# Batch 0 of an attention and MoE kernel: chunk 1 of w_in loaded before the second x, the order of TensorE's work changed, zero matmuls widened

## The chip, the core and the metric

The kernel runs on one core of a Trainium2 chip. Time is device microseconds (us) of that core; less is better. A profile is one execution of the program, taken by the hardware profiler. The engines have names used throughout: PE is TensorE's matmul, PEld its weight load, DVE is VectorE, ACT is ScalarE, POOL is GpSimd, SP is SyncE. Each has its own queue and works through it in order; engines wait for each other through semaphores.

## What is computed

Eight batches of x (8 heads, 512 positions, 64 values) attend to a state of 32 rows and the state attends to x; the 544 rows of each batch go through a two-layer network with SiLU.

```python
def _attn_ref(x, state):               # B, H, S, Ns, D = 8, 8, 512, 32, 64
    scores = scale * np.matmul(x, state.transpose(0, 1, 3, 2))
    ...                                # softmax over the state's rows: a
    xread = np.matmul(a, state)
    scores2 = scale * np.matmul(state, x.transpose(0, 1, 3, 2))
    ...                                # softmax over the positions: a2
    sread = np.matmul(a2, x)
    return np.concatenate([xread, sread], axis=2)

def _moe_ref(x, w_in, w_out):          # 4352 rows; w_in 512 x 2048, w_out 2048 x 512
    h = x @ w_in
    g = h * (1.0 / (1.0 + np.exp(-h)))
    return g @ w_out
```

## The kernel before

All matrix work is in bf16 with fp32 sums in PSUM. PSUM is used as eight named banks: o0, o1, w0, w1, h0, h1, a0, a1. The order of the program is written by hand; no scheduler moves anything, and semaphores follow from what each instruction reads and writes.

Batch b needs these steps. `cast_x` makes bf16 of the loaded x (eight casts, one for each kt and half); `x_T` transposes it on PE and `x_Te` copies the result to xT; `sc` makes the scores against the state, `ex` takes their exponentials on ACT, `norm_s` and `norm_m` divide by the sums. `a_T` transposes the normalised weights, with a copy to aT. Since the state has only 32 rows, the state is multiplied into w_in first: `w1_m(b, j)` makes chunk j (512 of the 2048 columns) of W1 from the state and chunk j of w_in, in two PSUM banks, and `w1_e` copies the two halves to SBUF. `W1x` is both, here with DVE copying bank a0 and ACT bank a1. `g1(b, ft)` then is two matmuls (one for each half) of W1's block ft with aT into bank h0 or h1, by turns, and ACT's SiLU into g; four blocks ft make one chunk. `G2(0, ft)` adds block ft of g times w_out into the four banks o0, o1, w0, w1, four matmuls. `sread_m`, `sread_n` and `sread_t` make the state's read of x, and x_T, sc and a_T share the banks a0 and a1 with it. `x_T`, `sc` and `ex` of two kt go together in batch 1 and later (`xTs`, `scs`, `exs`).

Batch 0 is the ramp: loads arrive, batch 0's network runs while batch 1's softmax and W1 are made, and PE takes all of it in the order in which the program has it. `warm(n, bk)` puts n matmuls of zeros, 128 columns wide, into a bank that is free. From phase 1 on (`phase(k, fill)`), PE goes through 64 G2 matmuls of batch k, step 16*tt+ft, and the table `fill` inserts the work of the next batches behind chosen steps: `att_tail(fill, b, s, a0, sg, dg)` puts the transposes a_T of batch b at step a0 and its sixteen g1 from step sg on, dg steps apart. In these phases ACT copies aT.

Loads: x of batch 0 goes out on SP's queue in four pieces. The weights, in four chunks each of w_in and w_out, and x of batches 1 and 2 go out on POOL's queue, whose DMA instructions convert fp32 to bf16 on the way for weights. POOL also works: two of batch 0's `norm_m` and the casts for kt 3 of x1 stand in the same queue, and a DMA issue behind them waits for them.

Of the kernel before, what the change touches and what calls it, by code (L numbers as in the profile page):

```python
# [9 lines left out]
BF16 = mybir.dt.bfloat16  # L10
# [9 lines left out]
def kernel(  # L20
# [8 lines left out]
    nc = tc.nc  # L29
# [8 lines left out]
        tc.tile_pool(name="psum", bufs=1, space=bass.MemoryType.PSUM)  # L38
    )

    zeros = pers.tile([128, 128], BF16, name="zeros")
    ident = pers.tile([128, 128], BF16, name="ident")
    st0_f = pers.tile([128, 128], FP32, name="st0_f")
    st_nat = pers.tile([128, B, 128], BF16, name="st_nat")
# [43 lines left out]
    def load_x(b, eng, kt=0, n=4):  # L88
        dst = x_f[b % 2][:, ds(kt, n)].rearrange("p k h e -> p (k h) e")
        eng.dma_start(dst, x_src(b, kt, n))  # L90
# [35 lines left out]
    def x_T(b, kt, bk):  # L126
        v = bf(bk).rearrange("p (k c t) -> p k c t", k=2, c=4)
        for c in range(4):
            nc.tensor.transpose(  # L129
                v[:, kt % 2, c, :], x_n[b % 2][:, kt, c, ds(2, 128)], ident[:]  # L130
            )

    def x_Te(b, kt, n, bk, eng):
        v = bf(bk).rearrange("p (k c t) -> p k c t", k=2, c=4)
        cp(eng, xT[b % 2][:, ds(kt, n)], v[:, ds(kt % 2, n)])
# [154 lines left out]
        cp(eng, t[:, c0:c1], bank[bk][:, c0:c1])  # L290
        (q or nc.sync).dma_start(o_dst(b, tt, c0, c1), t[:, c0:c1])

    def warm(n, bk):
        for i in range(n):
            nc.tensor.matmul(
                bank[bk][:, 0:128], zeros[:], zeros[:], start=True, stop=True,
                skip_group_check=True,
            )

    with tc.manual_schedule():  # L300
# [11 lines left out]
        load_wi(0)  # L312
        load_wo(0)
        load_st(1)
        load_x(1, nc.gpsimd, 0, 2)
        load_x(1, nc.gpsimd, 2, 2)
        warm(20, "o0")

        XB = ("o0", "o1", "w0", "w1")
        SB = ("h0", "h1", "a0", "a1")  # L320
# [6 lines left out]
        def G2(b, ft):  # L327
            for tt in range(4):
                g2(b, tt, ft, OB[tt])
# [22 lines left out]
        cast_x(0, "dve", (1,))  # L352
        st_T(0, "a1", "act", "dve")
        cast_x(0, "dve", (2, 3))
        for kt in range(KT):
            if kt < 3:
                x_T(0, kt + 1, XB[kt + 1])
                x_Te(0, kt + 1, 1, XB[kt + 1], ("act", "act", "dve")[kt])
            sc(0, kt, SB[kt])
            ex(0, kt, 1, SB[kt])  # L360
            if kt == 1:
                warm(6, "o0")
        norm_s(0, 0, 2)
        norm_m(0, "pool", 0, 2)
        norm_s(0, 2, 2)
        norm_m(0, "dve", 3, 1)
        norm_m(0, "pool", 2, 1)
        nc.scalar.preload_act_table(SILU)
        warm(10, "o0")
        w1_m(0, 0, ("w0", "w1"))  # L370
        w1_e(0, 0, ("w0", "w1"), ("act", "act"))
        a_T(0, (("a0", "dve"), ("a1", "dve")))
        load_wi(1)
        load_wo(1)
        load_wi(2)

# [7 lines left out]
        G2(0, 1)  # L384
        sread_t(0, "a1", "dve")
        G2(0, 2)
        cast_x(1, "dve", (0, 1, 2))
        cast_x(1, "pool", (3,))
        load_wo(2)
        load_wi(3)  # L390
        load_wo(3)
        load_x(2, nc.gpsimd)
        for b in range(2, B):
            load_st(b)
        xTs(1, 0, "dve")
        G2(0, 3)
        xTs(1, 1, "act")
        scs(1, 0)
        scs(1, 1)
        exs(1)  # L400
        norm_s(1)
        norm_m(1, "dve")

        W1x(0, 1, AB, DA)
        W1x(1, 0, HB, DA)
        nc.scalar.preload_act_table(SILU)
        a_T(1, (("a0", "dve"),))
        g1(0, 4)
        g1(0, 5)
        g1(0, 6)  # L410
        W1x(1, 1, AB, DA)
        g1(0, 7)
        G2(0, 4)
        g1(1, 0)
        G2(0, 5)
        g1(1, 1)
        G2(0, 6)
        W1x(0, 2, AB, DA)
        g1(1, 2)
        G2(0, 7)  # L420
        g1(1, 3)

        g1(0, 8)
        W1x(1, 2, AB, DA)
        g1(0, 9)
        g1(0, 10)
        g1(0, 11)
        G2(0, 8)
        g1(1, 4)
        G2(0, 9)  # L430
        g1(1, 5)
        G2(0, 10)
        W1x(0, 3, AB, DA)
        g1(1, 6)
        G2(0, 11)
        g1(1, 7)

        g1(0, 12)
        W1x(1, 3, AB, DA)
        g1(0, 13)  # L440
        g1(0, 14)
        G2(0, 12)
        g1(0, 15)
        G2(0, 13)
        g1(1, 8)
        G2(0, 14)
        g1(1, 9)
        G2(0, 15)
        g1(1, 10)
        for tt in range(4):  # L450
            o_e(0, tt, OB[tt], "dve")
        cast_x(2, "pool", (2, 3))
# [47 lines left out]
        add(fill, 8, L(sread_t, 1, "a1", "dve"))  # L500
        add(fill, 8, L(cast_x, 3, "pool"))
        att_head(fill, 2, 9, 17)
        att_tail(fill, 2, 20, 43, 46, 1.1)
        att_head(fill, 3, 48, 58)
        phase(1, fill)

        for k in range(2, 7):
            fill = {}
            if k + 2 < B:
                load_x(k + 2, nc.sync)  # L510
            att_tail(fill, k + 1, 0, 24, 28, 2.15)
            if k + 2 < B:
                add(fill, 0, L(cast_x, k + 2, "pool"))
                att_head(fill, k + 2, 42, 56)
            phase(k, fill)
# [45 lines left out]
```

## Time and profile before

| | us |
|---|---|
| median of 3 runs | 240.18 |
| lowest, highest | 239.5, 241.35 |
| the profiled execution | 239.66 |
| its span, first to last instruction | 237.9 |
| around the span (239.66 - 237.9) | 1.76 |
| busy in the span: PE, ACT, DVE, POOL | 222.2, 138.3, 83.8, 43.9 |

Times in the profile count from the start of the span. A row of a timeline is one or more equal instructions in sequence: start, time until the last of them ends, engine, source line, operation, the tiles written and read, their number, and in brackets the idle time of the engine ahead of it with what ended it. PE's matmuls overlap, so that eight of them can be shorter than eight times one; what one costs in a row is the distance of the starts. PEclk is the clock that TensorE was granted, as a share of 2.4 GHz; 0.50 is 1.2 GHz.

### The profile page before, as it was taken

To read this page: it belongs to the slowest core of one execution; us is meant where nothing else is said; L and a number is where in the kernel's file an instruction comes from. 1 tells how busy PE (TensorE), PEld (TensorE's weight loads), DVE (VectorE), ACT (ScalarE), POOL (GpSimd) and SP (SyncE) were. 2 spreads that over 40 slices of the span, in tenths; PEclk is the share of its full clock that TensorE was granted. 3 is DMA by queue.
4 is the path that set the end of the run, shared out by engine and by line. 5 is a ranking of instruction groups with operands and counts; after the bars stand their busy time and mean duration, and the time that the engine had idled before them with its cause. 6 is when DMAs were issued, how large, how long until landed. Compare 5 with 4: busy or idle time off the path is not lost.

```text
span 237.9 us, 4311 instructions
## 1 busy us (share of the span) xinstructions
PE 222.2 (93%) x1764; PEld 111.2 (47%) x1764; DVE 83.8 (35%) x162; ACT 138.3 (58%) x224; POOL 43.9 (18%) x79
## 2 busy tenths in 40 slices
PE   5797399999999999999999999999999999999993
PEld 4644143444544534453445444544454444466552
DVE  4626622116663164225423461436142711111110
ACT  3652756566467795668565766576657766533210
POOL 4648212000340007000700052003400300000000
PEclk9999679999999999999999999999999999999999
DMA  6999990007511053113411261117101121011112
GB/s 187 156 272 204 207 263 2 1 0 209 192 47 44 3 156 110 47 44 96 171 44 47 61 206 47 41 46 225 44 3 44 47 88 43 15 66 57 44 48 88
DMA packets 18309, 22.08 MB, mean 93 GB/s; under 512 B 3056, under 2 KB 13552, under 8 KB 18288
## 3 DMA queue, kind: packets, MB, share of 16 engines
q1 hardware_dynamic: 11040, 14.81, 19.0%
q0 software_dynamic: 6688, 6.52, 14.9%
q10 hardware_dynamic: 560, 0.46, 0.6%
q8 instruction: 14, 0.23, 0.4%
q14 instruction: 7, 0.06, 0.1%
HBM read 17.30 MB, written 8.91 MB: 110 GB/s over the span
## 4 chain that ended last, share of the span: by engine, by line
PE 85%; ACT 5%; DMA 4%; DVE 3%; issue 1%; POOL 0%; ACTq 0%
PE ps_o L270 44%; PE ps_h L246 24%; PE ps_w L270 3%; DMA w_in_sb<-in_moe_w_in_dram 3%; PE ps_h L257 3%; PE ps_a L129 3%; ACT aT L82 3%; PE ps_w L225 2%; PE ps_a L182 2%; DMA st_f<-in_state_dram 1%; PE ps_a L192 1%; PE ps_a L140 1%; PE ps_h L225 1%; ACT g L254 1%; PE ps_a L225 1%
## 5 line engine op out<-in xcount | busy, mean ns | idle before, releaser
L270 PE MATMUL ps_o<-w_out_sb,g 128*128 128x512 bf16 x480 | 131.2, 379 | 0.0
L254 ACT ACTIVATE g<-ps_h 128x512 bf16<-128x512 f32 x128 | 76.0, 598 | 47.3 <-PE ps_h L246 46.5
L246 PE MATMUL ps_h<-aT,W 128*128 128x512 bf16 x256 | 77.2, 389 | 2.1 <-ACT aT L82 1.6
L270 PEld LDWEIGHTS <-g 128*128 128x128 bf16 x512 | 47.5, 98 | 49.6 <-issue 2.9
L78 DVE COPY o_sb<-ps_o 128x512 f32<-128x512 f32 x30 | 20.5, 685 | 70.7 <-PE ps_o L270 70.7
L246 PEld LDWEIGHTS <-W 128*128 128x128 bf16 x256 | 25.1, 100 | 33.3 <-issue 8.0
L166 POOL TENSOR_TENSOR an<-en,rs 128x1024 bf16<-128x1024 bf16 (+2 forms) x8 | 13.3, 1665 | 96.2 <-DVE rs L162 96.2
L80 POOL CAST x_n<-x_f 128x256 bf16<-128x256 f32 x46 | 16.2, 400 | 39.9 <-PE ps_a L140 26.3
L78 DVE CAST W<-ps_w 128x512 bf16<-128x512 f32 x24 | 15.4, 683 | 1.8 <-PE ps_w L225 1.6
L82 ACT ACTIVATE W<-ps_h 128x512 bf16<-128x512 f32 x25 | 13.7, 603 | 0.5 <-PE ps_h L225 0.5
L78 DVE COPY xT<-ps_a 128x1024 bf16<-128x1024 bf16 x13 | 9.0, 690 | 11.5 <-PE ps_a L129 9.1
L265 ACT ACTIVATE g_s<-ps_h 128x256 bf16<-128x256 f32 x16 | 6.1, 383 | 11.6 <-PE ps_h L257 11.6
L161 DVE TENSOR_REDUCE rs<-en 128x32 f32<-128x1024 bf16 (+1 forms) x9 | 9.9, 1098 | 7.2 <-ACT en L151 7.2
L82 ACT ACTIVATE aT<-ps_a 128x1024 bf16<-128x1024 bf16 x6 | 6.1, 1023 | 10.4 <-PE ps_a L182 10.4
L129 PEld LDWEIGHTS <-x_n 128*128 128x128 bf16 x128 | 8.9, 103 | 6.9 <-DVE x_n L78 3.9
L78 DVE COPY sbd<-ps_a 64x128 bf16<-64x128 bf16 x15 | 4.3, 289 | 20.3 <-PE ps_a L118 20.1
L151 ACT ACT_TABLE_LOAD x7 | 9.0, 1283 | 3.2 <-PE ps_a L140 3.1
L257 PE MATMUL ps_h<-xsT,w_in_sb 128*128 128x256 bf16 x64 | 9.6, 273 | 0.0
L270 PE MATMUL ps_w<-w_out_sb,g 128*128 128x512 bf16 x32 | 9.5, 379 | 0.0
L78 DVE CAST W<-ps_a 128x512 bf16<-128x512 f32 x6 | 4.1, 690 | 14.7 <-PE ps_a L225 14.7
L129 PE MATMUL ps_a<-ident,x_n 128*128 128x128 bf16 x112 | 8.7, 219 | 0.6 <-DVE x_n L78 0.6
L151 ACT ACTIVATE en<-ps_a 128x512 bf16<-128x512 f32 (+1 forms) x16 | 8.4, 568 | 1.0 <-PE ps_a L140 0.9
(59 smaller groups left out, 140.5 us busy)
## 6 DMA issues: line engine op xcount, KB each, us to landing
out_dram<-o_sb SPq DMA_DIRECT2D x32, 256.0 KB, 2.3
x_f<-in_x_dram SPq DMA_DIRECT2D x5, 1024.0 KB, 6.7
w_in_sb<-in_moe_w_in_dram POOLq DMA_DIRECT2D x4, 512.0 KB, 10.1
w_out_sb<-in_moe_w_out_dram POOLq DMA_DIRECT2D x4, 512.0 KB, 9.9
x_f<-in_x_dram SPq DMA_DIRECT2D x4, 256.0 KB, 3.7
x_f<-in_x_dram POOLq DMA_DIRECT2D x2, 512.0 KB, 9.5
x_f<-in_x_dram POOLq DMA_DIRECT2D x1, 1024.0 KB, 15.6
out_dram<-o_sb ACTq DMA_DIRECT2D x1, 256.0 KB, 3.3
```

What stands on the lines that cost most here:

```text
L78: nc.vector.tensor_copy(dst, src)
L80: nc.gpsimd.tensor_copy(dst, src)
L82: nc.scalar.activation(dst, src, func=COPY, bias=0.0)
L129: nc.tensor.transpose(v[:, kt % 2, c, :], x_n[b % 2][:, kt, c, ds(2, 128)], ident[:])
L151: nc.scalar.activation(en[b % 2][:, :, :, ds(kt, n), :].rearrange("p c h k s -> p k (c h) s"), v[:, ds(kt % 2, n)], func=EXP, bias=0.0, sc ...
L161: nc.vector.tensor_reduce(v, en[b % 2][:, :, :, ds(kt, n), :], axis=AX, op=ADD)
L166: e.tensor_tensor(an[b % 2][:, :, :, ds(kt, n), :].rearrange("p c h k s -> p (c h) k s"), en[b % 2][:, :, :, ds(kt, n), :].rearrange("p c ...
L225: nc.tensor.matmul(bank[bks[half]][ds(32 * kt, 32), :], sbd[ds(64 * half, 64), b, kt, half, :], w_in_sb[ds(64 * half, 64), kt, ds(512 * j, ...
L246: nc.tensor.matmul(bk[:], W1[b % 2][:, half, ds(128 * ft, 128)], aT[b % 2][:, half, :, :], start=(half == 0), stop=(half == 1), skip_group ...
L254: nc.scalar.activation(g[b % 2][:, ft, :], bk[:], func=SILU, bias=0.0)
L257: nc.tensor.matmul(bk[:, 0:256], w_in_sb[:, kt, ds(128 * ft, 128)], xsT[:, kt, :, :, :], start=(kt == 0), stop=(kt == KT - 1), skip_group_ ...
L270: nc.tensor.matmul(bank[bk][:, c0:c1], src[:, ft, ds(128 * tt, 128)], w_out_sb[:, ft, c0:c1], start=(ft == 0), stop=(ft == 15), skip_group ...
```

## The change

The zeros tile becomes 512 columns wide and `warm` takes a width. In batch 0's softmax the loop is written out, with zero matmuls at other places and 28 in place of 20 at the start; ahead of the first W1 stand four of 512 columns in place of ten of 128, and two more stand between `a_T(0)` and the first g1. On POOL's queue chunk 1 of w_in is issued where x1's two halves were, and these behind the two `norm_m`. On PE, W1x(0,1), G2(0,3), g1(0,4) to g1(0,7) and W1x(1,0) now stand ahead of batch 1's transposes, and G2(0,4) to G2(0,7) behind its scores; W1x(1,0) uses a0 and a1 in place of h0 and h1; the rest of batch 0 is reordered. In the phases, `a_T` and the g1 get other steps: 42, 48 and 1.0 apart in phase 1 in place of 43, 46 and 1.1; 30 and 2.05 apart later in place of 28 and 2.15.

```diff
@@ -38,7 +38,7 @@
         tc.tile_pool(name="psum", bufs=1, space=bass.MemoryType.PSUM)
     )

-    zeros = pers.tile([128, 128], BF16, name="zeros")
+    zeros = pers.tile([128, 512], BF16, name="zeros")
     ident = pers.tile([128, 128], BF16, name="ident")
     st0_f = pers.tile([128, 128], FP32, name="st0_f")
     st_nat = pers.tile([128, B, 128], BF16, name="st_nat")
@@ -290,10 +290,10 @@
         cp(eng, t[:, c0:c1], bank[bk][:, c0:c1])
         (q or nc.sync).dma_start(o_dst(b, tt, c0, c1), t[:, c0:c1])

-    def warm(n, bk):
+    def warm(n, bk, w=128):
         for i in range(n):
             nc.tensor.matmul(
-                bank[bk][:, 0:128], zeros[:], zeros[:], start=True, stop=True,
+                bank[bk][:, 0:w], zeros[:, 0:128], zeros[:, 0:w], start=True, stop=True,
                 skip_group_check=True,
             )

@@ -312,9 +312,8 @@
         load_wi(0)
         load_wo(0)
         load_st(1)
-        load_x(1, nc.gpsimd, 0, 2)
-        load_x(1, nc.gpsimd, 2, 2)
-        warm(20, "o0")
+        load_wi(1)
+        warm(28, "o0")

         XB = ("o0", "o1", "w0", "w1")
         SB = ("h0", "h1", "a0", "a1")
@@ -352,25 +351,35 @@
         cast_x(0, "dve", (1,))
         st_T(0, "a1", "act", "dve")
         cast_x(0, "dve", (2, 3))
-        for kt in range(KT):
-            if kt < 3:
-                x_T(0, kt + 1, XB[kt + 1])
-                x_Te(0, kt + 1, 1, XB[kt + 1], ("act", "act", "dve")[kt])
+        warm(4, "w1")
+        x_T(0, 1, XB[1])
+        x_Te(0, 1, 1, XB[1], "act")
+        sc(0, 0, SB[0])
+        ex(0, 0, 1, SB[0])
+        warm(3, "w1")
+        x_T(0, 2, XB[2])
+        x_Te(0, 2, 1, XB[2], "act")
+        sc(0, 1, SB[1])
+        ex(0, 1, 1, SB[1])
+        x_T(0, 3, XB[3])
+        x_Te(0, 3, 1, XB[3], "dve")
+        warm(2, "o0")
+        for kt in (2, 3):
             sc(0, kt, SB[kt])
             ex(0, kt, 1, SB[kt])
-            if kt == 1:
-                warm(6, "o0")
         norm_s(0, 0, 2)
         norm_m(0, "pool", 0, 2)
         norm_s(0, 2, 2)
         norm_m(0, "dve", 3, 1)
         norm_m(0, "pool", 2, 1)
         nc.scalar.preload_act_table(SILU)
-        warm(10, "o0")
+        warm(4, "o0", 512)
         w1_m(0, 0, ("w0", "w1"))
         w1_e(0, 0, ("w0", "w1"), ("act", "act"))
         a_T(0, (("a0", "dve"), ("a1", "dve")))
-        load_wi(1)
+        warm(2, "o0", 512)
+        load_x(1, nc.gpsimd, 0, 2)
+        load_x(1, nc.gpsimd, 2, 2)
         load_wo(1)
         load_wi(2)

@@ -384,69 +393,68 @@
         G2(0, 1)
         sread_t(0, "a1", "dve")
         G2(0, 2)
-        cast_x(1, "dve", (0, 1, 2))
+        W1x(0, 1, AB, DA)
+        G2(0, 3)
+        g1(0, 4)
+        cast_x(1, "dve", (0, 1))
         cast_x(1, "pool", (3,))
+        g1(0, 5)
+        W1x(1, 0, AB, DA)
+        g1(0, 6)
+        cast_x(1, "dve", (2,))
         load_wo(2)
         load_wi(3)
         load_wo(3)
         load_x(2, nc.gpsimd)
         for b in range(2, B):
             load_st(b)
+        g1(0, 7)
         xTs(1, 0, "dve")
-        G2(0, 3)
         xTs(1, 1, "act")
         scs(1, 0)
         scs(1, 1)
         exs(1)
         norm_s(1)
         norm_m(1, "dve")
-
-        W1x(0, 1, AB, DA)
-        W1x(1, 0, HB, DA)
         nc.scalar.preload_act_table(SILU)
-        a_T(1, (("a0", "dve"),))
-        g1(0, 4)
-        g1(0, 5)
-        g1(0, 6)
-        W1x(1, 1, AB, DA)
-        g1(0, 7)
         G2(0, 4)
-        g1(1, 0)
         G2(0, 5)
-        g1(1, 1)
         G2(0, 6)
         W1x(0, 2, AB, DA)
-        g1(1, 2)
         G2(0, 7)
-        g1(1, 3)

         g1(0, 8)
-        W1x(1, 2, AB, DA)
         g1(0, 9)
+        a_T(1, (("a0", "dve"),))
         g1(0, 10)
+        W1x(1, 1, AB, DA)
         g1(0, 11)
         G2(0, 8)
+        g1(1, 0)
+        G2(0, 9)
+        g1(1, 1)
+        W1x(1, 2, AB, DA)
+        G2(0, 10)
+        g1(1, 2)
+        G2(0, 11)
+        g1(1, 3)
+        W1x(0, 3, AB, DA)
         g1(1, 4)
-        G2(0, 9)
         g1(1, 5)
-        G2(0, 10)
-        W1x(0, 3, AB, DA)
-        g1(1, 6)
-        G2(0, 11)
-        g1(1, 7)

         g1(0, 12)
+        g1(0, 13)
         W1x(1, 3, AB, DA)
-        g1(0, 13)
         g1(0, 14)
         G2(0, 12)
         g1(0, 15)
         G2(0, 13)
-        g1(1, 8)
+        g1(1, 6)
         G2(0, 14)
-        g1(1, 9)
+        g1(1, 7)
         G2(0, 15)
-        g1(1, 10)
+        for ft in range(8, 11):
+            g1(1, ft)
         for tt in range(4):
             o_e(0, tt, OB[tt], "dve")
         cast_x(2, "pool", (2, 3))
@@ -500,7 +508,7 @@
         add(fill, 8, L(sread_t, 1, "a1", "dve"))
         add(fill, 8, L(cast_x, 3, "pool"))
         att_head(fill, 2, 9, 17)
-        att_tail(fill, 2, 20, 43, 46, 1.1)
+        att_tail(fill, 2, 20, 42, 48, 1.0)
         att_head(fill, 3, 48, 58)
         phase(1, fill)

@@ -508,7 +516,7 @@
             fill = {}
             if k + 2 < B:
                 load_x(k + 2, nc.sync)
-            att_tail(fill, k + 1, 0, 24, 28, 2.15)
+            att_tail(fill, k + 1, 0, 24, 30, 2.05)
             if k + 2 < B:
                 add(fill, 0, L(cast_x, k + 2, "pool"))
                 att_head(fill, k + 2, 42, 56)
```

POOL's queue, from the first weight load on: the rows of before. w_in_sb and w_out_sb are the weights, an_74 is batch 0's normalised softmax, x_f_67 and x_n_69 are x of batch 1 before and after its cast.

```order
L96 DMA w_in_sb<-in_moe_w_in_dram 128x4x512
L101 DMA w_out_sb<-in_moe_w_out_dram 128x4x512
L104 DMA st_nat<-in_state_dram 128x2x64
L90 DMA x_f_67<-in_x_dram 128x4x256 x2
L166 TENSOR_TENSOR an_74<-en_72,rs_76 128x8x64
L166 TENSOR_TENSOR an_74<-en_72,rs_76 128x8x32
L96 DMA w_in_sb<-in_moe_w_in_dram 128x4x512
L101 DMA w_out_sb<-in_moe_w_out_dram 128x4x512
L96 DMA w_in_sb<-in_moe_w_in_dram 128x4x512
L80 CAST x_n_69<-x_f_67 128x4x64 x2
```

The same stretch of POOL's queue in the change:

```order
L96 DMA w_in_sb<-in_moe_w_in_dram 128x4x512
L101 DMA w_out_sb<-in_moe_w_out_dram 128x4x512
L104 DMA st_nat<-in_state_dram 128x2x64
L96 DMA w_in_sb<-in_moe_w_in_dram 128x4x512
L166 TENSOR_TENSOR an_74<-en_72,rs_76 128x8x64
L166 TENSOR_TENSOR an_74<-en_72,rs_76 128x8x32
L90 DMA x_f_67<-in_x_dram 128x4x256 x2
L101 DMA w_out_sb<-in_moe_w_out_dram 128x4x512
L96 DMA w_in_sb<-in_moe_w_in_dram 128x4x512
L80 CAST x_n_69<-x_f_67 128x4x64 x2
```

The second load of w_in and the two loads of x1 have changed places around the two multiplies; all that follows is as it was.

DVE's queue, from the state's read of batch 0 (xsT) to batch 1's aT_79, before. W_80 is W1 of batch 0 and W_81 of batch 1, xT_71, rs_77 and an_75 belong to batch 1's softmax, and ps_a_100 and ps_h_98 are banks a0 and h0.

```order
L78 COPY xsT<-ps_a_101 128x4x32
L78 CAST x_n_69<-x_f_67 128x4x64 x6
L78 COPY xT_71<-ps_a_100 128x1024
L161 TENSOR_REDUCE rs_77<-en_73 128x32
L162 RECIPROCAL rs_77<-rs_77 128x32
L166 TENSOR_TENSOR an_75<-en_73,rs_77 128x1024
L78 CAST W_80<-ps_a_100 128x512
L78 CAST W_81<-ps_h_98 128x512
L78 COPY aT_79<-ps_a_100 128x1024
```

The same stretch of DVE's queue in the change:

```order
L78 COPY xsT<-ps_a_101 128x4x32
L78 CAST W_80<-ps_a_100 128x512
L78 CAST x_n_69<-x_f_67 128x4x64 x4
L78 CAST W_81<-ps_a_100 128x512
L78 CAST x_n_69<-x_f_67 128x4x64 x2
L78 COPY xT_71<-ps_a_100 128x1024
L161 TENSOR_REDUCE rs_77<-en_73 128x32
L162 RECIPROCAL rs_77<-rs_77 128x32
L166 TENSOR_TENSOR an_75<-en_73,rs_77 128x1024
L78 CAST W_80<-ps_a_100 128x512
L78 COPY aT_79<-ps_a_100 128x1024
```

The casts of W1(0,1) and W1(1,0) have moved ahead of and between the casts of x1, and the cast behind the softmax multiply is now that of W1(0,2).

## Rows read from the trace of the kernel before

**Rows 1.** Stages: length, busy time of PE, PEld, DVE, ACT, POOL; PEclk, DMA, GB/s.

```profile
16.12:19.35 3.23, 3.23 (x47) 1.37 (x45) 1.71 (x6) 0.80 (x2) 2.13 (x4) 1.00 1.22 203
...
22.30:25.70 3.40, 0.93 (x14) 0.49 (x11) 0.00 (x0) 3.34 (x4) 1.03 (x3) 1.00 1.24 206
25.70:29.20 3.50, 1.05 (x15) 0.25 (x15) 3.43 (x5) 2.37 (x3) 1.15 (x2) 0.50 1.24 206
29.20:32.50 3.30, 3.28 (x14) 1.50 (x13) 1.26 (x2) 1.12 (x2) 0.71 (x1) 0.50 1.18 292
32.50:54.38 21.88, 21.49 (x130) 8.84 (x130) 4.34 (x7) 13.71 (x26) 1.43 (x4) 1.00 0.21 34
```

**Rows 2.** Timeline of PE, chosen rows up to 37 us.

```profile
0.99 2.32 PE L295 MATMUL ps_o<-zeros 128*128 128x128 bf16 x20 [0.99 <-DVE zeros L305]
...
11.35 0.63 PE L225 MATMUL ps_w<-w_in_sb,sbd 64*32 64x512 bf16 x8 [0.72 <-DMA w_in_sb<-in_moe_w_in_dram]
12.02 1.03 PE L182 MATMUL ps_a<-ident,an 128*128 128x128 bf16 x8
13.14 3.14 PE L246 MATMUL ps_h<-aT,W 128*128 128x512 bf16 x8
16.12 0.59 PE L270 MATMUL ps_o<-w_out_sb,g 128*128 128x512 bf16 x2
...
29.22 1.01 PE L182 MATMUL ps_a<-ident,an 128*128 128x128 bf16 x8 [2.45 <-DVE W L78]
30.03 2.69 PE L246 MATMUL ps_h<-aT,W 128*128 128x512 bf16 x6
...
33.44 0.59 PE L270 MATMUL ps_o<-w_out_sb,g 128*128 128x512 bf16 x2
33.87 0.59 PE L270 MATMUL ps_w<-w_out_sb,g 128*128 128x512 bf16 x2
...
36.98 0.41 PE L225 MATMUL ps_a<-w_in_sb,sbd 64*32 64x512 bf16 x8
```

**Rows 3.** Timelines of ACT and DVE, chosen rows up to 29 us.

```profile
12.03 1.09 ACT L82 ACTIVATE W<-ps_w 128x512 bf16<-128x512 f32 x2 [0.75 <-PE ps_w L225]
...
22.25 1.02 ACT L82 ACTIVATE xT<-ps_a 128x1024 bf16<-128x1024 bf16 x1 [5.33 <-PE ps_a L129]
...
24.58 1.09 ACT L151 ACTIVATE en<-ps_a 128x512 bf16<-128x512 f32 x2
...
18.93 2.41 DVE L78 CAST x_n<-x_f 128x256 bf16<-128x256 f32 x6
...
25.70 1.22 DVE L161 TENSOR_REDUCE rs<-en 128x32 f32<-128x1024 bf16 x1 [3.76 <-ACT en L151]
...
28.49 0.68 DVE L78 CAST W<-ps_a 128x512 bf16<-128x512 f32 x1
```

**Rows 4.** POOL's timeline; among it an issue at 11.91: KB landed, us to landing.

```profile
11.91 0.79 POOL L96 DMA_DIRECT2D w_in_sb<-in_moe_w_in_dram  x1
...
w_in_sb<-in_moe_w_in_dram POOLq DMA_DIRECT2D x1, 512.0 KB, 8.5
...
17.22 0.74 POOL L80 CAST x_n<-x_f 128x256 bf16<-128x256 f32 x2 [3.02 <-DMA x_f<-in_x_dram]
...
25.44 0.71 POOL L104 DMA_DIRECT2D st_nat<-in_state_dram  x1 [1.80 <-DMA w_in_sb<-in_moe_w_in_dram]
27.99 0.70 POOL L104 DMA_DIRECT2D st_nat<-in_state_dram  x1 [1.84 <-DMA w_out_sb<-in_moe_w_out_dram]
```

**Rows 5.** Groups from 33 to 54 us: busy us, mean ns, idle before.

```profile
L254 ACT ACTIVATE g<-ps_h 128x512 bf16<-128x512 f32 x20 | 11.5, 602 | 6.3 <-PE ps_h L246 6.3
```

**Rows 6.** Groups of DVE, from 18.8 to 21.4 us and from 56 to 60.

```profile
L78 DVE CAST x_n<-x_f 128x256 bf16<-128x256 f32 x6 | 2.4, 468 | 0.0
...
L78 DVE CAST x_n<-x_f 128x256 bf16<-128x256 f32 x4 | 0.9, 281 | 0.0
```

**Rows 7.** Waits of PE from 54 us on: us in total, times, longest.

```profile
PE ps_h L246 <- ACT aT L82: 1.6, 6, 0.4
```

## The prediction

> **What bounds the kernel now.** I read the page first. By its table of engines TensorE (PE) is busy for nearly the whole span and no other engine for two thirds of it. The view by stages says where the rest lies: from 22.30 to 25.70 PE works 0.93 of 3.40 us, from 25.70 to 29.20 1.05 of 3.50, while from 32.50 to 54.38 it works 21.49 of 21.88 [rows 1]. So two things can move the end: holes and low clock before phase 1 starts at 54.38, and small PE waits after it. The other engines are hidden under PE.
>
> What fills the holes is read from the PE timeline [rows 2] and the timelines of ACT and DVE [rows 3]. Batch 1's softmax is one chain: transposes, ACT's copy of xT at 22.25 (1.02 us), the load of the exp table behind it, two exps at 24.58 (1.09), DVE's sum at 25.70 with the reciprocal and the multiply behind it, a W cast at 28.49 (0.68), and only then PE's a_T at 29.22, which had waited 2.45. PE has nothing else in its queue: second-chunk work of batch 0 needs w_in's chunk 1, whose issue on POOL's queue stands behind both halves of x1 (issued 11.91, 8.5 us to landing, so 20.4), while x1 is whole at 17.2 [rows 4].
>
> **The clock.** The granted clock is 0.50 (1.2 GHz) from 25.7 to 32.5 [rows 1]; ahead of that PE had been mostly idle. At the start the column reads 1.00, but the rows contradict it: eight transposes take 1.03 us at 12.02, as at 29.22 under 0.50 (1.01), and eight W1 matmuls take 0.63 at 11.35 against 0.41 at 36.98, where the clock is 1.00 [rows 2]. So PE runs at the low level until g1 begins, and at the high one by 16.12, where two G2 matmuls take 0.43, as at 33.44 (to 33.87) [rows 2].
>
> **The change, part by part.** Times of the new kernel are on the old trace's axis.
>
> *To the first G2.* w_in's chunk 0 still lands at 11.3: nothing ahead of it on a queue changes. The softmax of batch 0 may end a little before that, so w1_m still starts at 11.35. What the zero matmuls can change is the clock there. If it is high by about 13 us: w1_m takes 0.41, ACT's two W copies (1.09 as at 12.03 [rows 3]) run 11.8 to 12.9, and g1 starts at 12.9 instead of 13.14. Four g1 of 0.43 over two banks, each bank freed by an activation of 0.60 [rows 5], put the third at 14.2, the fourth at 14.7 and G2 at 15.1 instead of 16.12. That is 1.0 us. If the clock rises only as it did before, the two wide zeros between a_T and g1 (0.43 us each at the low level: four times the 0.11 of a 128-column one, from 20 in 2.32 [rows 2]) start g1 at 13.7 and G2 at about 16.6: 0.5 lost. I take the first: the zeros ahead of w1_m grow from 36 x 128 columns to 37 x 128 plus 4 x 512, and 28 of them in place of 20 stand ahead of the first transpose.
>
> *The filled hole.* The 3.23 us from 16.12 to 19.35, G2, the state's read and two G2, all of it PE work [rows 1], now run 15.1 to 18.3. w_in chunk 1 and x1 change places in the DMA queue, and a chunk is read as 512 by 512 fp32 values, as many as x1 has; so I let them change landings: chunk 1 at 17.2, x1 at 20.4 [rows 4]. Chunk 1 is then there in time, and W1x(0,1) (0.45 with its gaps), G2(0,3) (0.87), g1 4 and 5 (0.87), W1x(1,0) (0.45) and g1 6 and 7 (0.87) follow, to 21.8.
>
> *The chain, put behind that.* DVE now does in order: W cast (ends 19.4), four x casts, W cast, two x casts. Six x casts took 2.41 us at 18.93 [rows 3], 0.40 each, so: 21.0, 21.7, 22.4. Transposes 0.45, ACT's copy 1.02 to 23.95, table and exps, 22.25 + 1.02 to 24.58 + 1.09 before, 2.4 to 26.35, then DVE as from 25.70 to 28.49 plus the offset of the cast: multiply done 29.25, W cast of W1x(0,2) 29.85. That last cast was not behind the softmax before; g1 8 is queued on PE behind it. PE meanwhile does the transposes and scores, G2 4 to 6 (2.6), W1x(0,2) (0.45) and G2 7 (0.87): to 28.0, then waits 1.85. So g1 8 starts at 29.9.
>
> The x casts have bounds. With DVE undisturbed they cost 0.28, beside POOL's DMA issues 0.47 on the mean of that stretch [rows 6]: chain 0.7 earlier to 0.4 later. I take 0.40, the step measured for this very work. The Trainium skill (SBUF — State Buffer, section "SBUF: two separate sides") says that DVE and GpSimd lock one shared port pair for a whole instruction, so that one blocks the other, descriptor writing included. By it each of the six casts could wait out a POOL issue of up to 0.79 us, which would put the sum 2.3 us higher; this trace agrees only in that the casts are longer there: the mean is 0.47, so the row decides.
>
> *What is gained at 29.9.* At 30.03 the old kernel starts g1 4. The new one starts g1 8, having done four g1 (1.73), four G2 (3.46) and one W1x (0.45) more, and the a_T (0.45) less: 5.2, plus 0.13. The low clock of 30.0 to 32.5, when PE was full, goes too: 1.25. Against it, new waits that I work out from the order: a_T(1) writes a0 and W1x(1,1) must wait for DVE's copy of it (0.4); g1 12 comes right after W1x(0,3), g1(1,4) and g1(1,5), so it waits for an ACT copy and an activation (0.55); three g1 in a row at the end run at ACT's pace (0.3). 1.25 together, bounds 0.4 and 2.0; the old stage's idle 0.39 (21.88 less 21.49 [rows 1]) goes. Sum: 5.2 + 0.13 + 1.25 - 1.25 + 0.39 = 5.7 us earlier at phase 1. Chunk 2 of w_in landed by 25.4, that of w_out by 28.0 [rows 4]; they are asked for at about 26.9 and 32.9.
>
> *The phases.* PE waits for ACT's copy of aT six times, 1.6 us in total [rows 7], once in each of phases 1 to 6. The new step numbers put g1 six G2 matmuls behind a_T in place of three or four: 0.65 and 0.43 us more cover, against waits of at most 0.41. All of it goes. Phase 1's last g1 moves from step 62 to 63, just ahead of the next W1 pair on the same bank: up to 0.1 back. 1.5 us. If the cover were missing, it is worth nothing.
>
> *Sum.* 5.7 + 1.5 = 7.2 us. The profiled execution took 239.66 us (span 237.9 plus 1.76), so 232.5. The median of the runs, 240.18, is 0.5 above it, and they spread from 239.5 to 241.35. I work from the profiled execution and leave 232.5 as it is.
>
> **The rivals.**
>
> - *The clock rises as late as before.* For it: zeros, 36 of them, did not lift it before 11.35 [rows 2], and after 10 us the two orders are much alike. Against: more zero work early. G2 at 16.6 in place of 15.1, all behind it 1.5 later: 234.0.
> - *The clock falls in the new wait at 28 to 29.9.* For it: PE idleness of that kind preceded the fall at 25.7. Against: PE did 0.93 us of work from 22.30 to 25.70 then [rows 1], and now a wait of 1.85 has 3.9 us of solid work ahead of it. At the low level for as long as in the old trace (6.8 us), the work takes twice its time: 3.4 us, 235.9.
> - *The phase waits move instead of going* (ACT held up elsewhere): 1.5 less, 234.0.
> - *Slower: x1 comes late.* Its issue now stands on POOL behind the softmax multiplies and in the DMA queue between weight chunks. If the chunks behind it share its time, its last half lands with them, at 28.0 (chunk 2 of w_out [rows 4]) in place of 20.4. PE's queue stops at the transposes at 22.5, with nothing beside them; POOL's two casts add 0.74: 6.2 us lost, and the clock falls as it did at 25.7, 3.4 more: 242.1. It decides from a landing at 26 us on, where the loss passes the 7.7 between forecast and median. Against it: loads landed in the order of their issue, x1 (17.2), then chunk 1 (20.4).
>
> **How the numbers follow.** Forecast case 52%, its own range 231.2 to 233.4 (casts, and the bounds 0.4 and 2.0 of the new waits). Late clock 22%, falling clock 14%, phases unchanged 6%, x1 late 6%, split between the price above, which is within 1% of the median, and later landings. The range 231.0 to 236.2 takes in all but the last and some tails, about 0.85. About 1% is what a measurement here can tell from no change: faster by more than that means under 237.8. All cases but x1 late do it, less a tail of 1%: 0.93; within 1% 0.04; slower 0.03.
>
> **What would show it.** Eight W1 matmuls in about 0.41 us at 11.4, and G2 from 15.1, confirm the clock; 0.63 and 16.6 the late rise. PE should show W1x(0,1) near 18.3 without a DMA wait, one wait of about 1.9 us ending on DVE's W cast near 29.9, granted clock 1.00 throughout, and phase 1 from 48.7. The waits for aT should be gone from phases 1 to 6. A PE wait for x_n, or a transpose later than 23, would speak for the slower rival; a granted clock of 0.50 anywhere after 16 us would make the prediction too low.

## The result, and the profile after

| | before | changed |
|---|---|---|
| median, us | 240.07 (4 runs) | 232.03 (4 runs) |
| lowest to highest | 239.5 to 241.35 | 230.78 to 234.53 |
| the profiled execution | 239.66 | 231.27 |
| its span | 237.9 | 229.4 |

The ratio of changed to before is 0.9641, 95% interval 0.9568 to 0.9713: 7 to 10 us less. The ratios here and below leave out runs that lie more than 1.5% above a kernel's fastest (here the one at 234.53), so they can differ from the ratio of two medians. The forecast was 232.5 with a range of 231.0 to 236.2. In the profiled executions 8.5 us of span are gone: phase 1 starts at 48.21 in place of 54.38, 6.2 us, and the rest of the program takes 2.3 us less. Of the 6.2 us, 1.5 are gained by the first G2 (14.63 in place of 16.12) and 4.7 between it and phase 1.

The view by stages of the changed kernel (columns as in [rows 1]; the stages are cut at the starts of PE's pieces):

```profile
17.95:21.38 3.43, 3.43 (x30) 1.24 (x30) 2.27 (x7) 2.17 (x5) 1.54 (x4) 1.00 1.19 211
21.38:23.79 2.41, 1.70 (x33) 1.41 (x32) 1.02 (x3) 2.29 (x5) 2.41 (x4) 1.00 1.22 169
23.79:27.80 4.01, 3.96 (x29) 1.50 (x26) 1.81 (x3) 3.97 (x5) 2.61 (x4) 1.00 1.17 174
27.80:29.45 1.65, 0.06 (x1) 0.00 (x1) 1.59 (x2) 0.00 (x1) 0.70 (x1) 1.00 1.22 202
29.45:48.21 18.76, 17.70 (x109) 7.49 (x112) 5.62 (x9) 12.05 (x22) 2.14 (x5) 1.00 0.51 106
```

Where [rows 1] had seven microseconds with 2 of PE work and then 3.3 us at a granted clock of 0.50, PE now works without a hole from 17.95 to 21.38 and from 23.79 to 27.80, with 0.7 us of waits between the two, and the clock reads 1.00 throughout. What is left is one hole of 1.65 us before 29.45.

PE's timeline in the changed kernel, chosen rows:

```profile
1.19 3.17 PE L295 MATMUL ps_o<-zeros 128*128 128x128 bf16 x28 [1.19 <-DVE zeros L305]
...
4.80 0.64 PE L295 MATMUL ps_w<-zeros 128*128 128x128 bf16 x4
5.42 0.61 PE L129 MATMUL ps_o<-ident,x_n 128*128 128x128 bf16 x4
...
6.85 0.40 PE L129 MATMUL ps_w<-ident,x_n 128*128 128x128 bf16 x4 [0.31 <-DVE x_n L78]
...
11.03 0.41 PE L225 MATMUL ps_w<-w_in_sb,sbd 64*32 64x512 bf16 x8 [1.71 <-DMA w_in_sb<-in_moe_w_in_dram]
11.37 0.62 PE L182 MATMUL ps_a<-ident,an 128*128 128x128 bf16 x8
...
12.28 1.18 PE L246 MATMUL ps_h<-aT,W 128*128 128x512 bf16 x4
...
14.63 0.59 PE L270 MATMUL ps_o<-w_out_sb,g 128*128 128x512 bf16 x2
...
17.95 0.41 PE L225 MATMUL ps_a<-w_in_sb,sbd 64*32 64x512 bf16 x8
...
21.38 1.05 PE L129 MATMUL ps_a<-ident,x_n 128*128 128x128 bf16 x16
...
29.45 1.04 PE L246 MATMUL ps_h<-aT,W 128*128 128x512 bf16 x4 [1.59 <-DVE W L78]
...
31.71 0.41 PE L225 MATMUL ps_a<-w_in_sb,sbd 64*32 64x512 bf16 x8 [0.35 <-DVE aT L78]
...
39.95 1.08 PE L246 MATMUL ps_h<-aT,W 128*128 128x512 bf16 x4 [0.35 <-ACT g L254]
```

The clock shows in the durations: four transposes take 0.61 us at 5.42 and 0.40 at 6.85, so TensorE went from 1.2 to 2.4 GHz near 6 us, where in [rows 2] it did so only during g1, between 13.14 and 16.12; eight W1 matmuls take 0.41 at 11.03 (0.63 before) and eight transposes 0.62 at 11.37 (1.03). W1x(0,1) at 17.95 waits for no DMA. Then the three waits that the prediction had worked out from the order: 1.59 for DVE's W cast, 0.35 for the copy of aT, 0.35 for an activation.

The chain of batch 1, from the timelines of DVE, ACT and POOL of the changed kernel:

```profile
19.03 0.89 DVE L78 CAST x_n<-x_f 128x256 bf16<-128x256 f32 x4
...
21.22 0.49 DVE L78 CAST x_n<-x_f 128x256 bf16<-128x256 f32 x2
...
22.47 1.02 ACT L82 ACTIVATE xT<-ps_a 128x1024 bf16<-128x1024 bf16 x1
...
25.92 1.22 DVE L161 TENSOR_REDUCE rs<-en 128x32 f32<-128x1024 bf16 x1 [3.21 <-ACT en L151]
...
28.71 0.68 DVE L78 CAST W<-ps_a 128x512 bf16<-128x512 f32 x1
...
19.84 0.74 POOL L80 CAST x_n<-x_f 128x256 bf16<-128x256 f32 x2 [5.68 <-DMA x_f<-in_x_dram]
```

The chain itself is no earlier than before (the sum at 25.92, 25.70 in [rows 3]): x1 is whole at 19.84 in place of 17.2. The gain in this stretch is what PE does beside it and ahead of it.

### The profile page after: what moved, and what is told of

It is laid out like the page before. It is cut to its first block, busy times and chain, and to the rows that moved or that the text cites. A ratio compares the mean times of both kernels' runs of the same rounds, so it can differ in the third digit from the quotient of the medians.

```text
span 229.4 us, 4300 instructions
## 1 busy us (share of the span) xinstructions
PE 215.9 (94%) x1744; PEld 109.1 (48%) x1771; DVE 83.1 (36%) x162; ACT 137.9 (60%) x224; POOL 43.9 (19%) x79
## 4 chain that ended last, share of the span: by engine, by line
PE 88%; DMA 4%; ACT 2%; DVE 2%; issue 2%; POOL 0%
PE ps_o L270 47%; PE ps_h L246 23%; PE ps_h L257 3%; PE ps_w L270 3%; DMA w_in_sb<-in_moe_w_in_dram 3%; PE ps_a L129 3%; PE ps_w L225 2%; PE ps_a L182 2%; DMA st_f<-in_state_dram 1%; PE ps_h L225 1%; PE ps_a L192 1%; PE ps_a L140 1%; ACT g L254 1%; PE ps_a L225 1%; ACT L151 1%
## 5 line engine op out<-in xcount | busy, mean ns | idle before, releaser
L270 PE MATMUL ps_o<-w_out_sb,g 128*128 128x512 bf16 x461 | 126.4, 379 | 2.1 <-issue 1.6
L246 PE MATMUL ps_h<-aT,W 128*128 128x512 bf16 x250 | 73.9, 380 | 2.6 <-DVE W L78 1.6
L270 PEld LDWEIGHTS <-g 128*128 128x128 bf16 x512 | 46.9, 98 | 49.1 <-issue 3.6
L246 PEld LDWEIGHTS <-W 128*128 128x128 bf16 x256 | 24.4, 98 | 32.7 <-issue 2.9
L82 ACT ACTIVATE W<-ps_h 128x512 bf16<-128x512 f32 x24 | 13.1, 603 | 0.5 <-PE ps_h L225 0.5
L257 PEld LDWEIGHTS <-w_in_sb 128*128 128x128 bf16 x64 | 6.2, 98 | 4.1
```

Of the source, the lines that this page charges most:

```text
L82: nc.scalar.activation(dst, src, func=COPY, bias=0.0)
L246: nc.tensor.matmul(bk[:], W1[b % 2][:, half, ds(128 * ft, 128)], aT[b % 2][:, half, :, :], start=(half == 0), stop=(half == 1), skip_group ...
L257: nc.tensor.matmul(bk[:, 0:256], w_in_sb[:, kt, ds(128 * ft, 128)], xsT[:, kt, :, :, :], start=(kt == 0), stop=(kt == KT - 1), skip_group_ ...
L270: nc.tensor.matmul(bank[bk][:, c0:c1], src[:, ft, ds(128 * tt, 128)], w_out_sb[:, ft, c0:c1], start=(ft == 0), stop=(ft == 15), skip_group ...
```

## The experiments

Each kernel ran beside the kernel before, in three groups; the medians of before in them were 239.85 (p1, z1, l1, o1), 240.13 (a1, n1, n3, n2) and 239.93 (z2, l2, n4, n5). Ratios are to these; two kernels of different groups are best compared by their ratios.

| label | what it is | median, us | ratio to before, 95% |
|---|---|---|---|
| p1_phases_only | before, new step numbers | 237.37 | 0.9891 (0.9856 to 0.9926) |
| z2_zeros_only | before, new zeros | 240.78 | 0.9991 (0.9947 to 1.0036) |
| o1_old_order | changed, old PE order in batch 0 | 237.49 | 0.9885 (0.9833 to 0.9938) |
| z1_old_zeros | changed, old zeros | 232.91 | 0.9711 (0.9671 to 0.9751) |
| l1_old_loads | changed, old load order | 234.52 | 0.9751 (0.9700 to 0.9802) |
| a1_after_again | changed | 231.97 | 0.9680 (0.9625 to 0.9734) |
| n3_more_zeros | changed, ten wide zeros | 231.58 | 0.9650 (0.9614 to 0.9686) |
| l2_old_loads_zeros | n3, old load order | 233.33 | 0.9722 (0.9677 to 0.9767) |
| n1_act_w02 | changed, W1x(0,2) copied by ACT | 230.42 | 0.9602 (0.9566 to 0.9638) |
| n2_wi0_first | n1, w_in chunk 0 issued earlier | 234.25 | 0.9756 (0.9713 to 0.9800) |
| n4_both | n1 and n3 | 229.67 | 0.9583 (0.9543 to 0.9623) |
| n5_order | n4, two pieces moved | 229.46 | 0.9579 (0.9535 to 0.9623) |

### The phases alone (p1)

The edit is the last two hunks of the change, put into the kernel before:

```diff
-        att_tail(fill, 2, 20, 43, 46, 1.1)
+        att_tail(fill, 2, 20, 42, 48, 1.0)
-            att_tail(fill, k + 1, 0, 24, 28, 2.15)
+            att_tail(fill, k + 1, 0, 24, 30, 2.05)
```

> The kernel before with the two new rows of step numbers alone (a_T and g1 in phases 1 to 6). Theory A, sized by the wait rows: the six waits for aT (1.6 us) go, 238.5 from 240.07. Theory B, sized by the distance of the aT copies from phase to phase (24.73 us before, 24.33 in the changed kernel, five phases, and 0.3 in phase 1): 2.3 us, 237.7. Rival: the waits move elsewhere in the phase, 240.0.

It measured 237.37, 2.5 us below before. That is theory B (whose size had been read from the changed kernel's trace), and more than the 1.5 us of the prediction. ACT's copies of aT, one in each phase, show the period. First two rows of before, then the same phases of the changed kernel:

```profile
91.74 1.02 ACT L82 ACTIVATE aT<-ps_a 128x1024 bf16<-128x1024 bf16 x1 [1.48 <-PE ps_a L182]
116.47 1.02 ACT L82 ACTIVATE aT<-ps_a 128x1024 bf16<-128x1024 bf16 x1 [1.80 <-PE ps_a L182]
```

```profile
85.26 1.02 ACT L82 ACTIVATE aT<-ps_a 128x1024 bf16<-128x1024 bf16 x1 [1.47 <-PE ps_a L182]
109.64 1.02 ACT L82 ACTIVATE aT<-ps_a 128x1024 bf16<-128x1024 bf16 x1 [1.80 <-PE ps_a L182]
133.97 1.02 ACT L82 ACTIVATE aT<-ps_a 128x1024 bf16<-128x1024 bf16 x1 [1.80 <-PE ps_a L182]
```

The wait for aT in these two phases of before:

```profile
92.81 0.59 PE L246 MATMUL ps_h<-aT,W 128*128 128x512 bf16 x2 [0.19 <-ACT aT L82]
117.55 0.59 PE L246 MATMUL ps_h<-aT,W 128*128 128x512 bf16 x2 [0.25 <-ACT aT L82]
```

A phase takes 24.73 us before. After, the first of these takes 24.38, 0.35 less where the idle row showed 0.19, and the second 24.33, 0.40 less where it showed 0.25. The wait rows count PE's idle time from the modelled end of the last matmul, 0.38 us after its start, while the next could have started 0.216 after it. So each such wait costs some 0.16 us more than its row says, about 1.0 us for six. Over p1's four periods from its second copy of aT to the sixth, 97.35 us pass, as in the changed kernel; before it was 98.94.

A little comes back. The end of phase 1, where the last g1 now stands one step ahead of the next W1 on banks h0 and h1, first before, then changed:

```profile
84.38 0.56 PE L225 MATMUL ps_h<-w_in_sb,sbd 64*32 64x512 bf16 x8
84.88 3.19 PE L270 MATMUL ps_o<-w_out_sb,g 128*128 128x512 bf16 x14
```

```profile
77.69 0.78 PE L225 MATMUL ps_h<-w_in_sb,sbd 64*32 64x512 bf16 x8
```

0.78 in place of 0.56 us: 0.22 us, where the prediction had up to 0.1.

### The order of PE's work (o1)

The changed kernel, with the lines from W1x(0,1) and the casts of x1 to the end of batch 0's stretch, ahead of its output copies, as they were before; loads, zeros and phases stay as changed.

> The changed kernel (its loads, zeros and phases) with the program order of before from the x1 casts to the end of batch 0. Theory: the order is what fills the hole, so PE again idles from about 20 to 29, the clock falls and the time goes back to that of before less the phases and what is left of the early clock: 236.5 to 238. Rival: zeros and loads carry the gain, 232 to 233.

It measured 237.49, the same as the phases alone gave the kernel before. So zeros and loads gain nothing that these runs can tell under the old order (the runs of o1 and p1 spread over 2.5 and 3.6 us), as the theory had it. PE's timeline of o1:

```profile
23.44 0.41 PE L140 MATMUL ps_a<-sbd,xT 128*128 128x64 bf16 x8 [0.88 <-ACT xT L82]
25.34 1.11 PE L225 MATMUL ps_a<-w_in_sb,sbd 64*32 64x512 bf16 x8 [1.50 <-ACT en L151]
25.85 1.03 PE L225 MATMUL ps_h<-w_in_sb,sbd 64*32 64x512 bf16 x8
29.33 1.01 PE L182 MATMUL ps_a<-ident,an 128*128 128x128 bf16 x8 [2.45 <-DVE W L78]
```

The same hole with the same waits as before, 0.88, 1.50 and 2.45, and behind it the low level: eight transposes in 1.01 us. In this execution the early clock had been lost as well, in a wait of 2.40 us ahead of W1, and G2 started only at 16.84; so the trace shows what the order does, not what an early clock that lasts is worth under it.

### The zeros (z1, z2) and the spread of the changed kernel (a1)

z1 puts the zero matmuls of before into the changed kernel:

```diff
-        warm(28, "o0")
+        warm(20, "o0")
...
-        warm(4, "w1")
-        warm(3, "w1")
-        warm(2, "o0")
+        warm(6, "o0")
-        warm(4, "o0", 512)
+        warm(10, "o0")
...
-        warm(2, "o0", 512)
```

> The changed kernel with the zero matmuls of before (20, 6 and 10 of 128 columns at their old places, none of 512). Theory: the clock rises as late as before, eight W1 matmuls at about 11.3 take 0.63 us, G2 starts about 1.0 to 1.5 us later than 14.6 and all behind it moves along: 233.0 to 233.6 against 232.0. Rival: the zeros change nothing, the clock's rise is luck of the run: 232.0, with G2 at 14.6.

z1 measured 232.91, about 0.9 us above the changed kernel; its ratio, 0.9711, lies within the interval of a1's (0.9625 to 0.9734), so that the medians alone do not show a difference. In its trace the clock rose even later than before, near 17 us:

```profile
10.74 0.63 PE L225 MATMUL ps_w<-w_in_sb,sbd 64*32 64x512 bf16 x8 [0.32 <-DMA w_in_sb<-in_moe_w_in_dram]
...
16.31 1.06 PE L270 MATMUL ps_o<-w_out_sb,g 128*128 128x512 bf16 x2
17.16 0.83 PE L270 MATMUL ps_w<-w_out_sb,g 128*128 128x512 bf16 x2
```

G2 starts at 16.31 there, 1.7 later than in the changed kernel's trace; its span of 231.7 is 2.3 longer. That is what the new zeros were worth between these two traces, one execution of each. The old zeros do not always leave the clock low, though. In p1, which has them and runs the kernel of before up to phase 1, the clock was up by the first W1 (0.63 us in the trace of before), and down again by G2 (two matmuls in 0.99 us at 15.89):

```profile
10.15 0.41 PE L225 MATMUL ps_w<-w_in_sb,sbd 64*32 64x512 bf16 x8
```

And the medians differ by less than these traces, because the changed kernel does not always get what its best traces show:

> The changed kernel again, for its spread from run to run beside the variants of this group. Theory: the late or falling clock is what spreads it. Runs whose granted clock over the span is 0.997 or more lie near 231; runs with about 0.985 have one fall of 6.8 us and lie 3.4 us higher; runs with 0.993 or 0.990 lie 1.5 to 2 us higher. Rival: time and granted clock are unrelated.

a1's six runs fall into two groups: 230.72, 230.85 and 231.12 with a mean granted clock of 0.997 to 1.000, and 232.82, 233.20 and 234.01 with 0.989 to 0.992. So the runs with a low stretch lie some 2 to 3 us higher. The low stretch can be seen in l1, below. The Trainium skill (TensorE: Matmul & The Clock Gate, section "Part 1: The HAM clock gate") says that the moment of the rise differs from run to run of one kernel; the two traces of the changed kernel agree. The four transposes that took 0.61 us at 5.42 in the first took 0.40 in a1's:

```profile
5.62 0.40 PE L129 MATMUL ps_o<-ident,x_n 128*128 128x128 bf16 x4 [0.25 <-DVE x_n L78]
```

The clock need not be the whole of the spread. A mean clock leaves out what lies ahead of the first recorded change (z1's execution has 1.000, with the low level until 17 us). And w_in's chunk 0, issued between 4.09 and 4.34 us in all traces but n2's, took from 5.6 us (a1, n1, p1) to 8.5 (l2) and 8.8 (z2) to land. The shortest is reached with either load order, the two longest are with the old one. Where it lands late, W1 and G2 start late at any clock. How much of the spread is due to it was not tested.

z2 puts all of the new zeros, with the written-out softmax, into the kernel before.

> The kernel before with the new zero matmuls and the written-out softmax of batch 0 alone; its loads, its later order and its phases kept. Theory: G2 starts up to 1 us earlier, but the hole from about 21 to 29 stays, the clock falls in it, and x1's chain behind it moves with the casts: 239.1 to 240.1. Rival: the early clock is worth as much here as in the changed kernel: 238.5 or less.

The ratio is 0.9991, no difference, and the median of all twelve runs is 0.9 us above before's: no gain. In its profiled execution, its longest, the clock was up near 8 us (four score matmuls in 0.28 us) and down again for the wide zeros, ahead of the wait for chunk 0, and for the first W1:

```profile
8.76 1.90 PE L295 MATMUL ps_o<-zeros 128*128 128x512 bf16 x4
12.97 0.63 PE L225 MATMUL ps_w<-w_in_sb,sbd 64*32 64x512 bf16 x8 [2.32 <-DMA w_in_sb<-in_moe_w_in_dram]
```

The chunk itself landed 1.6 us later than in the trace of before. So this trace has neither an early clock that lasts nor an early G2 (18.62). Why an early clock that does last would be worth nothing here no trace shows; the theory, that batch 1's chain takes it back, was only argued.

### The load order (l1, l2)

l1 issues x1 ahead of chunk 1 of w_in again, with the changed kernel's PE order:

```diff
-        load_wi(1)
+        load_x(1, nc.gpsimd, 0, 2)
+        load_x(1, nc.gpsimd, 2, 2)
         warm(28, "o0")
...
-        load_x(1, nc.gpsimd, 0, 2)
-        load_x(1, nc.gpsimd, 2, 2)
+        load_wi(1)
         load_wo(1)
```

> The changed kernel with the load order of before (both halves of x1 ahead of chunk 1 of w_in), its PE order kept. Theory: W1x(0,1), at 17.95 in the changed kernel, waits for the chunk until about 20.4, 2.4 us, and the chain through DVE shifts with it: 234.4 against 232.0. Rival: the wait of 1.59 us ahead of g1 8 absorbs most of it, 232.8. If the clock falls in the new hole, another 3.4 on top: 237.8.

The number came as expected, 234.52, but the trace does not show the expected cause; it is of the fastest run, 232.66, while the other three lie near 234.6. Three rows of PE's timeline of l1:

```profile
10.88 0.41 PE L225 MATMUL ps_w<-w_in_sb,sbd 64*32 64x512 bf16 x8 [1.88 <-DMA w_in_sb<-in_moe_w_in_dram]
11.22 1.03 PE L182 MATMUL ps_a<-ident,an 128*128 128x128 bf16 x8
...
19.46 0.41 PE L225 MATMUL ps_a<-w_in_sb,sbd 64*32 64x512 bf16 x8
```

W1 ran at the high level after a hole of 1.88 us, and the transposes right behind it at the low one. This clock stretch made G2 1.3 us late (15.92), so chunk 1, which landed at 19.4 (issued at 10.62, 8.8 us), was hardly waited for. The run did not tell load order from clock. l2 was to do so: the same edit on the kernel with ten wide zeros (n3).

> The kernel with ten wide zeros, with x1 loaded ahead of chunk 1 of w_in as before: the load order alone, without the fall of the clock that came with it in the earlier run. Theory: W1x(0,1) waits for the chunk from about 17.9 to 19.4, 1.5 us: 233.1 against 231.6. Rival: the order of these two loads is worth nothing once PE's order is changed: 231.6.

It measured 233.33 against n3's 231.58, 1.75 us; n3 ran in another group, and the intervals of the two ratios still touch (0.9677 and 0.9686). Its PE waits up to 48 us have a row that n3 and the changed kernel lack:

```profile
PE ps_a L225 <- DMA w_in_sb<-in_moe_w_in_dram: 0.9, 1, 0.9
```

That is W1x(0,1) waiting for chunk 1, with 0.16 more that the row does not count; in this execution G2 had also started late, at 16.36, since chunk 0 took 8.5 us to land (5.9 in n3's trace). From the first G2 to g1 8 pass 15.84 us, against 14.82 in n3 and in the changed kernel, and 15.03 in l1. So load order is worth about 1.75 us by medians, which is little more than their noise, and 0.2 and 1.0 us directly in the two traces; whether it also delays chunk 0 these runs don't tell.

### Filling the hole ahead of W1 (n3), and one that misfired (n2)

```diff
-        warm(4, "o0", 512)
+        warm(10, "o0", 512)
```

> The changed kernel with ten wide zero matmuls in place of four ahead of the first W1. Theory: PE's hole of 1.7 us ahead of the landing of chunk 0 of w_in, in which the clock fell in two of the three traces with the new zeros and the chunk's wait of 1.9 and 2.4 us, is filled at the high level; eight W1 matmuls take 0.41 us and a_T 0.6 in the trace, fewer runs with a low clock, median about 231.2. Rival: where the clock is low, ten of them last 4.3 us and hold up W1 by 1 to 1.5 us: 233.

n3 measured 231.58, 0.4 below a1, with a narrower spread: six runs from 230.91 to 232.58, all with a granted clock of 0.998 or more. Its PE timeline:

```profile
8.20 2.32 PE L295 MATMUL ps_o<-zeros 128*128 128x512 bf16 x10
10.45 0.41 PE L225 MATMUL ps_w<-w_in_sb,sbd 64*32 64x512 bf16 x8
11.16 0.62 PE L182 MATMUL ps_a<-ident,an 128*128 128x128 bf16 x8 [0.30 <-POOL an L166]
```

The hole is gone and the clock holds. In l2's trace, which has the same ten, the clock had fallen near 8 us, and the ten brought it up again ahead of W1 (0.41 us there):

```profile
9.06 3.38 PE L295 MATMUL ps_o<-zeros 128*128 128x512 bf16 x10
```

The gain in the median is smaller than the 0.8 expected, and a single pair of medians with this spread does not size it.

n2 issues chunk 0 of w_in ahead of the state's cast on POOL, in n1's kernel:

```diff
-        cp("pool", st_nat[:, 0, :], st0_f[:])
         load_wi(0)
+        cp("pool", st_nat[:, 0, :], st0_f[:])
```

> The kernel of n1 with chunk 0 of w_in issued ahead of the state's cast on POOL, about 2.5 us earlier. Theory: the chunk lands before batch 0's softmax is done, PE's hole ahead of W1 goes, and since a_T then waits for the softmax at about 11 us, G2 starts 0.3 us earlier: 230.7. Rival: x of batch 0 shares the transfer time with the chunk, its four pieces land up to 2.5 us later and the softmax with them: 233.

It lost 3.8 us against n1. Chunk 0 was issued at 1.44 in place of 4.29 us. PE's timeline of n2, the transposes of batch 0:

```profile
8.88 0.55 PE L129 MATMUL ps_w<-ident,x_n 128*128 128x128 bf16 x4 [2.48 <-DVE x_n L78]
...
11.13 0.61 PE L129 MATMUL ps_w<-ident,x_n 128*128 128x128 bf16 x4 [1.49 <-DVE x_n L78]
```

The last two pieces of x0 land late (the four took 5.0 us in the median, 3.7 in n1): the rival, larger than it was priced. G2 started at 18.55 there and at 14.13 in n1. A low clock behind the new holes goes with it (mean 0.982 to 0.983 in three of its four runs), but the fourth, with 0.999, took longest, 234.84; so the low clock does not explain the loss. The order in which w_in's first chunk follows x0 is not slack.

### The last hole (n1, n4, n5)

```diff
-        W1x(0, 2, AB, DA)
+        W1x(0, 2, AB, ("act", "act"))
```

> The changed kernel with both copies of W1x(0,2) given to ACT, so that none stands behind the softmax multiply on DVE. Theory: the wait of 1.59 us ahead of g1 8 is that cast alone; ACT copies at 27.2 and 27.7, g1 8 starts at 28.4 in place of 29.45, and a_T behind it is ready in time: 1.0 us less, 231.0. Rival: a_T, whose input leaves DVE at 28.8, or ACT with one copy more takes up the wait: 232.0.

n1 measured 230.42, 1.55 below a1, more than the 1.0 expected. Part of that is runs that kept the clock: five of its six have 0.996 or more, three of a1's. In the traces the stretch from the first G2 to phase 1 takes 32.47 us (14.13 to 46.60), in a1 33.64 (14.43 to 48.07): 1.2 us is the line's own. Its timeline has a_T at 28.64 without a wait, where the changed kernel has it at 30.32:

```profile
28.64 0.61 PE L182 MATMUL ps_a<-ident,an 128*128 128x128 bf16 x8
...
30.11 0.41 PE L225 MATMUL ps_a<-w_in_sb,sbd 64*32 64x512 bf16 x8 [0.42 <-DVE aT L78]
```

n4 takes n1 and n3 together:

> Both copies of W1x(0,2) on ACT, and ten wide zeros in place of four. Theory: the two are in different places and add up: 230.4 less 0.4, near 230.0, with no run above 231. Rival: the median stays at 230.4 because the runs of the first alone already kept the clock.

229.67, six runs from 229.49 to 230.49. n5 then moves G2(0,8) ahead of W1x(1,1), and W1x(0,3) ahead of g1(1,3) with G2(0,11) behind it:

> The last with G2(0,8) moved ahead of W1x(1,1) and W1x(0,3) ahead of g1(1,3), so that PE has work while DVE copies aT and while ACT works through W1(0,3). Theory: the waits of 0.42 and 0.35 us at about 30 and 39 go, 0.6 to 0.8 less: 229.4. Rival: ACT's row of activations is the bound there and the waits move to the next g1: 230.0.

229.46, 0.2 below n4, which is less than the runs differ among themselves; from the first G2 to phase 1 its trace takes 31.87 us and n4's 32.33. The wait for the copy of aT is gone from its list of PE waits, but those for an activation are not:

```profile
PE ps_h L246 <- ACT g L254: 0.8, 3, 0.3
```

So the rival holds for that part: between 30 and 48 us the row of activations sets the rest. n4 and n5 beat both kernels; which of the two is better their medians don't tell.

## Why the prediction was right

The forecast case happened, and its mechanism is shown: PE's order fills the hole (o1 takes it away and the time goes back to that of the phases alone), chunk 1's place in the queue lets W1x(0,1) start without a wait (0.2 and 1.0 us lost in the traces of l1 and l2 without it), the zeros raise the clock early (the durations at 6 and 11 us), and the phases are a part by themselves (p1). What the zeros and the load order are worth in the medians is less sure than the rest. In the profiled execution the sum came out 8.4 us against 7.2, and against medians 8.0. By stretch of the span it was 1.5 us to the first G2, 4.7 from there to phase 1 and 2.3 behind it; the sum had 1.0, 4.7 and 1.5.

That the median, 232.03, came so near to 232.5 is in part luck. Of the ten runs of the changed kernel (the first four and a1) five lie between 230.72 and 231.27, where the sum was too small, and five between 232.78 and 234.53, with the low clock that the sum had left to the rivals. The median lies between the two groups. Point by point:

- *To the first G2*: 14.63, forecast 15.1. w_in's chunk 0 landed 0.3 earlier than in the trace of before. And I let g1 wait for both W copies; its first matmul needs only the first, so g1 began at 12.28 and not at 12.9.
- *The filled hole*: W1x(0,1) at 17.95 (18.3), no wait; x1 at 19.84 (20.4).
- *The chain*: four x casts took 0.89 us and two 0.49, 0.22 to 0.25 each. I had taken 0.40 from [rows 3]; the lower bound was nearer, and itself too high: 0.28 in [rows 6] is the mean duration of casts that overlap, and the four there took 0.9 together. What made the six slower before is open. With casts this short PE did all sixteen transposes of x1 at 21.38, straight behind g1 7 and without a wait, so PE's queue and not the casts set the start of the chain. g1 8 started at 29.45 (29.9), after a wait of 1.59 (1.85) for the cast named. The Trainium skill (SBUF — State Buffer, section "SBUF: two separate sides") would have put the casts up to 2.3 us higher beside POOL's DMA issues; two casts ran at 21.22 while POOL issued at 21.25, and took 0.49, so this trace does not bear that out. The Trainium skill ties the lock there to DVE operations in a 2-port mode; whether these casts are such, no run here shows.
- *The new waits*: 0.35, 0.35 and 0.26 where 0.4, 0.55 and 0.3 stood.
- *Phase 1* at 48.21 (48.7): 6.2 us earlier, forecast 5.7.
- *The phases*: the mechanism was right, the term mis-sized: 1.5 in the sum, 2.3 in the trace and 2.5 in p1. What was wrong in it is "1.6 us in total [rows 7]", the idle of the wait rows taken for the cost of the wait; 0.2 us came back at the end of phase 1, where 0.1 stood.
- *The rivals*: x1 late did not happen. The phase waits did not move: no row of PE waiting for ACT's aT is left. The two on the clock are real, but as what happens to single runs: of a1's six, three have a low stretch. For the first I had read from one trace that 36 zeros did not lift the clock before 11.35; in p1 the same 36 did (W1 at 10.15). What I had as "falls in the wait at 28 to 29.9" is not seen in any trace of the changed kernel; the fall that traces of its variants show is earlier: in the hole ahead of the first W1 (l1, o1), or among x0's transposes and scores (z2, l2). Which of the two a run of the changed kernel at 233 or 234 has had, its time and mean clock alone don't say; that stays open.

## What to carry to other kernels

Give an in-order engine work that its data already allow before it comes to a chain that it must wait for, and load for that work first: the order was worth 5.5 us with loads and zeros in place (o1 against the changed kernel), while zero matmuls alone gave nothing (z2), and nor did zeros and loads together under the old order (o1 against p1). When a cast or copy that the next matmul needs is queued behind a long chain on its engine, look for an engine that is idle there (n1, 1.2 us in the traces for one line). And size a wait on PE by the distance of the same event from period to period, not by the idle time in its row.

## What the runs showed of the hardware that I had not expected

In all eleven traces with the new zeros TensorE was at the high level by 7 us (in n5 by 4.25); in the three with the old ones it rose near 10 us (p1), between 13 and 16 (before) and near 17 (z1). It did not always stay there. In l1 and o1 it fell in the hole ahead of W1, 1.88 and 2.40 us with work on both sides, while the changed kernel's first trace kept it through 1.71. But in l2 it fell near 7.8 us and in z2 near 8.7, among transposes and scores, with single waits of at most 0.67 us between them. So no length of a single wait tells here whether the clock holds. A wait row of PE understates a wait by 0.16 us, the modelled tail of a 512-column matmul. And the granted clock column reads 1.00 ahead of the first change that the profiler recorded, whatever the durations say: there only the durations tell.
